# Regrouping a batch one output unit sooner, with three small moves at the start, middle and end

## The chip, the cores and the metric

The kernel runs on one core of one Trainium2 chip. The metric is the device time of one execution in microseconds (us), the median over runs. The core has TensorE (PE, matmuls; PEld is its weight load), VectorE (DVE), ScalarE (ACT), GpSimd (POOL) and SyncE (SP), and 16 DMA engines, which the queues of SP, ACT and POOL feed.

## The reference

A squared-ReLU attention, followed by a gated feed-forward block. All inputs and outputs are float32.

```
q, k, v: 8 batches x 12 heads x 448 x 64
scores = q k^T / sqrt(64);  attn = max(scores, 0)^2 / 448
x = attn v, heads side by side: 3584 tokens x 768
gate = max(x w_gate, 0);  val = x w_val        (768 -> 1536)
out = (gate * val) w_out                       (1536 -> 768)
```

## The kernel before

Everything is computed in bfloat16 with float32 sums. The matmuls mostly use quarters of the PE array (`mm4`: four matmuls of 64 rows by 64 columns side by side).

**One batch's attention.** k and q come as 448 rows of 64 numbers per head (tiles `kn`, `qn`, two of each, used in turn) and are needed transposed: tile `kqT` (`T_b`) holds k and q with the 64 numbers on the partitions, two heads one above the other (a pair). Six pairs make three quads. Scores are made in 21 tiles (seven per quad, `tile_of`), each 128x896 in two PSUM banks; `relu2` takes them out with a ReLU on ACT (line 211) and a square on DVE (line 212). When a quad's seven tiles are done, `values` multiplies them by v (tile `vn`) into `x`.

**Three ways to the transpose.** The first batch is transposed on PE into PSUM, pair by pair (`transposes`, line 201), and copied by DVE (line 202). The second is too, as three quads. From the third batch on, `dma_transposes(b, t)` is used, once for k (t = 0) and once for q (t = 1): DVE regroups the batch's tile into `kr` or `qr` (line 177), and SP issues four DMA transposes (line 180).

**The order.** Nothing is left to a scheduler: every instruction is pinned, so each engine works in the order in which the program names its instructions. The feed-forward work of one batch is the frame: 12 units of the gate and value matmuls (`gv_units`, 12 steps each) and 6 or 8 output units (`out_units`, 12 steps each, two per block of 128 tokens). `spread(units, events)` walks through the units step by step and runs an event, such as a score tile of the next batch, when its place (unit, step) has come. Events are sorted by place; those with the same place keep the order of the list. For the second batch the list of units is ten gate and value units (0 to 9) and six output units (10 to 15). Its last score tile falls on (12, 8).

**Banks.** Gate, value and output units take two PSUM banks in turn: `acc` alternates between banks 6, 7 and 4, 5. A unit can start when the ACT and DVE instructions of the unit before the last have emptied its banks: for an output unit an ACT copy (line 310) and a DVE addition (line 311). Score tiles use banks 0 to 3, and in the first batch 4 and 5 too.

**Loads.** Loads of k, q, v and the weights are issued by POOL (`dma_in`, line 116) and follow each other in its queue. `hold(b)` makes POOL copy an element of the last transposed k and q (line 431), so that what POOL issues behind it starts after these transposes. The stores of an output block are issued by SP, two per block.

**The first batch** (`first_batch`) starts with matmuls on a tile of zeros, then the transposes of the first two pairs (one bank for k and q of a pair), five more such matmuls, and the score tiles. **The end** (`out_pieces`) makes the last block in pieces of 384, 192 and 192 columns; their stores are issued by SP, POOL, and SP with ACT.

Of the kernel before, what the change touches and what calls it, by code (L numbers as in the profile page):

```python
# [10 lines left out]
BF16 = mybir.dt.bfloat16  # L11
AF = mybir.ActivationFunctionType
# [4 lines left out]
def kernel(  # L17
# [22 lines left out]
    nc = tc.nc  # L40

    B, H, S, D = q.shape
# [22 lines left out]
    banks = psum.tile([128, 8, 512], FP32, name="ps")  # L65

    HALVES = [(c, slice(c * 64, c * 64 + 64)) for c in range(2)]

    def pin(ins):
        return tc.keep_in_program_order(ins)  # L70
# [4 lines left out]
    def mm2(o, l, r, start, stop):  # L75

        for c, p in HALVES:
            mm(o[p], l[:, p], r, start, stop)
# [10 lines left out]
    ident = const.tile([128, 128], BF16, name="ident")  # L89
    pin(nc.vector.memset(ident, 0.0))  # L90
    kn_b = [const.tile([128, H, 4, D], BF16, name=f"kn{i}") for i in range(NB)]
    qn_b = [const.tile([128, H, 4, D], BF16, name=f"qn{i}") for i in range(NB)]


    def pair_of(b, slot):
        qd, c = divmod(slot, 2)
        return slot if b == 0 else qd + c * NQ
# [17 lines left out]
    def dma_in(o, i):  # L115
        pin(nc.gpsimd.dma_start(out=o, in_=i))  # L116
# [19 lines left out]
    def load_qk(b, h0=0, h1=H):  # L136
        load_nat(kn_b[b % NB], k, b, h0, h1)
        load_nat(qn_b[b % NB], q, b, h0, h1)

    def load_v(b):  # L140
        for c, p in HALVES:
            if b == 0:
                src = v[b].rearrange("(g c h) s d -> c h g s d", c=2, h=2)[c]
                dst = v_b[b % NB][p].rearrange("p (g h) i d -> p h g i d", h=2)
                parts = [(dst[:, h2], src[h2]) for h2 in range(2)]
            else:
                parts = [(v_b[b % NB][p], v[b, c * HP:c * HP + HP])]
            for dst, src in parts:
                dma_in(dst[:, :, 0:4, :], src[:, 0:256, :].rearrange("g (j i) d -> j g i d", i=4))
                dma_in(dst[:, :, 4:7, :], src[:, 256:448, :].rearrange("g (j i) d -> j g i d", i=3))  # L150
# [19 lines left out]
    T_b = [const.tile([128, 2, HP, S], BF16, name=f"kqT{i}") for i in range(NB)]  # L170

    def dma_transposes(b, t):


        n = b % NB
        nat, grp = ((kn_b[n], kr), (qn_b[n], qr))[t]
        pin(nc.vector.tensor_copy(grp.rearrange("p i (h d) -> p i h d", d=D), nat.rearrange("p h i d -> p i h d")))
        for i in range(4):
            r = 128 if i < 3 else 64
            pin(nc.sync.dma_start_transpose(out=T_b[n][:, t, :, i * 128:i * 128 + r], in_=grp[0:r, i, :]))  # L180
# [14 lines left out]
    def transposes(b, hp, bank):  # L195

        ps = bank.bitcast(BF16).rearrange("p (t c) -> p t c", t=2)
        for t, nat in enumerate((kn_b[b % NB], qn_b[b % NB])):
            for i in range(4):
                for h2, half in HALVES:  # L200
                    pin(nc.tensor.transpose(ps[half, t, i * 128:i * 128 + 128], nat[:, 2 * hp + h2, i, :], ident))  # L201
        pin(nc.vector.tensor_copy(T_b[b % NB][:, :, hp, :], ps[:, :, 0:S]))  # L202

    def transpose_quad(b, qd):
        ps = sc_later()
        for c in range(2):
            transposes(b, pair_of(b, 2 * qd + c), ps[:, c, :])

    def relu2(src, dst):
        r = rpool.tile([128, 2, S], BF16, name="r_sb")  # L210
        pin(nc.scalar.activation(r, src, AF.Relu))  # L211
        pin(nc.vector.tensor_tensor(dst, r, r, ALU.mult))  # L212
# [8 lines left out]
    def tile_of(b, n, ps):  # L221

        qd, i = divmod(n, NC)
        T = T_b[b % NB]
        a = i * 128 if i < 4 else (i - 4) * 128 + 64
        mm4([ps[:, r, :S] for r in range(2)], lambda r, c: T[:, 0, pair_of(b, 2 * qd + c), a:a + 64],
            lambda r, c: T[:, 1, pair_of(b, 2 * qd + c), :], True, True)
        return ps[:, :, :S], attn_of(b, qd)[:, 2 * i:2 * i + 2, :]

    def value_passes(b, qd, ps, i0, i1):  # L230

        attn, v_sb = attn_of(b, qd), v_b[b % NB]
        for i in range(i0, i1):
            mm4([ps[:, r, :S] for r in range(2)], lambda r, c: v_sb[:, 2 * qd + c, i, :],
                lambda r, c: attn[:, 2 * i + c, :], i == 0, i == NC - 1)

    def exchange(b, qd):
        a = slice(2 * qd, 2 * qd + 2)
        for (_, p), (_, other) in zip(HALVES, HALVES[::-1]):
            pin(nc.vector.tensor_copy(x_of[b][1][p, a, :], x_of[b][0][other, a, :]))  # L240
# [7 lines left out]
    def idle_matmuls(ps, n):  # L248

        for _ in range(n):  # L250
            mm2(ps[:, :S], blank[:, 0:128], blank, True, True)
# [29 lines left out]
    def segment_rows(b0, s):  # L281

        b, s = b0 + s // 7, s % 7
        r = out[b * S:(b + 1) * S, :]
        i, half = divmod(s, 2)
        if half:
            return r[256:448, :].rearrange("(j i) m -> i j m", i=3)[i]
        return r[0:256, :].rearrange("(j i) m -> i j m", i=4)[i]

    def store(b0, t, o_sb, c0, c1, engines):  # L290
        for s in range(2):
            pin(engines[s].dma_start(out=segment_rows(b0, 2 * t + s)[:, c0:c1],  # L292
                                     in_=o_sb[s * 64:s * 64 + 64, c0:c1]))
# [22 lines left out]
    def out_pieces(b0, t):  # L316

        hT = hT_of[b0]
        o_sb = opool.tile([128, d_model], FP32, name="o_sb")
        cuts = [0, OH, OH + OH // 2, d_model]  # L320
        turn = [acc(), acc()]
        for n, (c0, c1) in enumerate(zip(cuts, cuts[1:])):
            o_ps = turn[n % 2][:, n // 2, :c1 - c0]
            for kf in range(KF):
                mm2(o_ps, hT[:, kf, bass.ts(t, 128)], wo_sb[kf // 6][:, kf % 6, c0:c1], kf == 0, kf == KF - 1)
            pin(nc.scalar.activation(out=o_sb[:, c0:c1], in_=o_ps, func=AF.Copy))  # L326
            store(b0, t, o_sb, c0, c1, ((nc.sync, nc.sync), (nc.gpsimd, nc.gpsimd), (nc.sync, nc.scalar))[n])

    STRAIGHT = [(e, hp) for e in range(2) for hp in range(HP)]

# [32 lines left out]
    def first_batch(units):  # L363


        def passes(u, n):
            for _ in range(n):
                units[u].pop(0)()

        def bank(n):  # L370
            return banks[:, n, :]

        def tile(n, at=None):
            todo.append(tile_of(0, n, sc_first() if at is None else banks[:, at:at + 2, :]))

        todo = []

        def scored():
            relu2(*todo.pop(0))

        idle_matmuls(bank(6), 12)
        transposes(0, 0, bank(6))
        transposes(0, 1, bank(7))
        idle_matmuls(bank(4), 5)
        tile(0)
        tile(1)
        both = banks[:, 6:8, :]
        for n in range(2, 19):
            tile(n)
            if n in (3, 5, 7, 9):  # L390
                hp = n // 2 + 1
                idle_matmuls(bank(6 + hp % 2), 2)
                transposes(0, hp, bank(6 + hp % 2))
            if n in (12, 17):
                value_passes(0, n // 14, both, 0, NC)
            scored()
            if n in (12, 17):
                qd = n // 14
                pin(nc.vector.tensor_copy(x_of[0][0][:, 2 * qd:2 * qd + 2, :], both[:, :, :S]))  # L399
        tile(19)  # L400
        scored()
        passes(0, 4)
        scored()
        tile(20, 0)
        scored()
        value_passes(0, 2, both, 0, 4)
        scored()
        passes(1, 4)
        value_passes(0, 2, both, 4, NC)
        exchange(0, 0)  # L410
        exchange(0, 1)
        pin(nc.scalar.activation(x_of[0][0][:, 4:6, :], both[:, :, :S], AF.Copy))
        exchange(0, 2)
        for n in range(4):
            for u in range(2):
                passes(u, 2)
# [4 lines left out]
    def values_event(b, qd):  # L421
        return lambda: values(b, qd, sc_later())
# [4 lines left out]
    def hold(b):  # L427

        flag = const.tile([128, 2], BF16, name="flag")
        for t in range(2):  # L430
            pin(nc.gpsimd.tensor_copy(flag[:, t:t + 1], T_b[b % NB][:, t, HP - 1, S - 1:S]))
# [20 lines left out]
    def evenly(units, u0, u1, events):  # L452
# [6 lines left out]
    units = gv_units(0)  # L459
    first_batch(units)  # L460
    load_qk(2)
    load_v(2)
    new_x(1)
    units = units[2:] + out_units(0)
    todo = events_of(1)
    spread(units, [(2, 6, transposes_event(1, 0)), (2, 6, transposes_event(1, 1)), (2, 10, transposes_event(1, 2)),
                   (3, 0, todo.pop(0))] + evenly(units, 3, 13, todo) +
           [(13, 8, lambda: dma_transposes(2, 0)), (14, 2, values_event(1, 2)),
            (14, 8, lambda: dma_transposes(2, 1)), (14, 8, lambda: hold(2))])
    for b in range(2, B):  # L470
        new_x(b)
        units = gv_units(b - 1) + out_units(b - 1)
# [37 lines left out]
```

## Time and profile before

| | us |
|---|---|
| median of 3 runs (420.43 to 422.28) | 421.97 |
| the profiled execution | 420.63 |
| its span, first to last instruction | 418.9 |
| PE busy in the span (98%) | 409.2 |
| DVE busy (58%) | 243.2 |
| ACT busy (56%) | 236.6 |
| POOL busy (15%) | 60.8 |

The times of single instructions below come from the profiled execution, which took 1.73 us more than its span. The granted clock of TensorE was 1.000. In the profile's lines the first two numbers are the start and the duration in us; "x4" is a number of instructions that were merged; the bracket at the end tells how long the engine was idle before, and what ended that. SPq and ACTq are the engines' DMA issues. In the table of windows the columns are the stretch, its length, the busy time (with the number of instructions) of PE, PEld, DVE, ACT and POOL, the granted clock, the share of the DMA engines and GB/s.

### The profile page before, as it was taken

How to read it: one execution, taken by the hardware profiler on the slowest of the kernel's cores; microseconds unless marked ns; L12 is line 12 of the kernel's file. 1: busy time of each engine (PE TensorE's matmuls, PEld its weight loads, DVE VectorE, ACT ScalarE, POOL GpSimd, SP SyncE). 2: the span in 40 equal slices, each digit the busy share in tenths (PEclk: the TensorE clock that was granted, in tenths of full speed). 3: DMA queues.
4: the chain of work that ended last, by engine and by line, in shares of the span. 5: the costliest groups of instructions: out<-in, count | busy, mean ns of one | idle time of the engine just before them, and what ended most of it. 6: DMA issues, size and time to landing. Idle time of an engine off the chain costs nothing.

```text
span 418.9 us, 19287 instructions
## 1 busy us (share of the span) xinstructions
PE 409.2 (98%) x8858; PEld 355.3 (85%) x8858; DVE 243.2 (58%) x422; ACT 236.6 (56%) x345; POOL 60.8 (15%) x93
## 2 busy tenths in 40 slices
PE   8899999999999999999999999999999999999996
PEld 4467677877887778877788899999999999999995
DVE  4985677436765666557565576557565555642221
ACT  3962886256764666565664756656555666632222
POOL 8823500053005000320004000020000000000001
PEclk9999999999999999999999999999999999999999
DMA  9999999789959960596316972271504100130014
GB/s 159 182 200 196 201 207 196 131 141 194 162 132 144 147 120 4 104 189 92 69 41 122 191 85 56 55 129 40 98 12 108 39 3 4 40 79 2 3 41 115
DMA packets 86033, 44.33 MB, mean 106 GB/s; under 512 B 54304, under 2 KB 82464, under 8 KB 85952
## 3 DMA queue, kind: packets, MB, share of 16 engines
q0 software_dynamic: 46976, 23.47, 42.7%
q1 hardware_dynamic: 38624, 19.39, 22.7%
q8 instruction: 69, 1.13, 1.1%
q10 hardware_dynamic: 352, 0.25, 0.2%
q14 instruction: 12, 0.10, 0.1%
HBM read 47.19 MB, written 11.01 MB: 139 GB/s over the span
## 4 chain that ended last, share of the span: by engine, by line
PE 91%; DVE 4%; DMA 2%; SPq 1%; issue 0%; ACT 0%; POOL 0%; POOLq 0%; DVEq 0%
PE ps L73 90%; DVE attn L212 2%; PE ps L201 1%; DMA kr<-in_k_dram 1%; SPq L180 1%; DMA kqT<-qr 1%; DVE kqT L202 1%; DVE x L399 0%; ACT r_sb L211 0%; DVE x L240 0%; DVE hT L278 0%; DVE kn L128 0%; POOL out_dram L292 0%; ACT g_sb L277 0%; POOLq L505 0%
## 5 line engine op out<-in xcount | busy, mean ns | idle before, releaser
L73 PE MATMUL ps<-x,gv 64*64 64x448 bf16 x4608 | 242.7, 349 | 0.4 <-ACT r_sb L211 0.3
L73 PEld LDWEIGHTS <-gv 64*64 64x64 bf16 x4608 | 192.7, 107 | 28.7 <-issue 2.1
L211 ACT ACTIVATE r_sb<-ps 128x896 bf16<-128x896 f32 x168 | 151.5, 924 | 56.8 <-PE ps L73 53.1
L212 DVE TENSOR_TENSOR attn<-r_sb 128x896 bf16<-128x896 bf16 x168 | 103.8, 624 | 80.0 <-ACT r_sb L211 79.6
L73 PE MATMUL ps<-wo,hT 64*64 64x384 bf16 (+2 forms) x2664 | 123.3, 321 | 0.8 <-issue 0.8
L73 PEld LDWEIGHTS <-hT 64*64 64x64 bf16 (+1 forms) x2664 | 105.2, 107 | 9.6 <-issue 1.6
L278 DVE TENSOR_TENSOR hT<-ps,g_sb 128x448 bf16<-128x448 f32 x96 | 59.7, 622 | 44.6 <-ACT g_sb L277 42.8
L277 ACT ACTIVATE g_sb<-ps 128x448 bf16<-128x448 f32 x96 | 51.9, 542 | 56.8 <-PE ps L73 56.2
L73 PE MATMUL ps<-kqT 64*64 64x448 bf16 x672 | 70.2, 351 | 3.3 <-ACT r_sb L211 2.2
L116 POOL DMA_DIRECT2D vn<-in_v_dram x36 | 23.4, 667 | 171.9 <-PE ps L73 156.1
L310 ACT ACTIVATE o_sb<-ps 128x384 f32<-128x384 f32 x54 | 26.4, 489 | 29.8 <-PE ps L73 29.3
L311 DVE TENSOR_TENSOR o_sb<-ps,o_sb 128x384 f32<-128x384 f32 x54 | 30.0, 555 | 19.7 <-ACT o_sb L310 19.4
L73 PEld LDWEIGHTS <-kqT 64*64 64x64 bf16 x672 | 29.7, 107 | 10.4 <-issue 3.7
L73 PE MATMUL ps<-attn,vn 64*64 64x448 bf16 x672 | 37.9, 349 | 0.0
L73 PEld LDWEIGHTS <-vn 64*64 64x64 bf16 x672 | 27.6, 107 | 4.2 <-issue 0.3
L244 ACT ACTIVATE x<-ps 128x448 bf16<-128x448 f32 x21 | 11.4, 544 | 29.8 <-PE ps L73 29.8
L245 DVE CAST x<-ps 128x448 bf16<-128x448 f32 x21 | 13.1, 625 | 15.4 <-PE ps L73 15.4
L240 DVE COPY x<-x 64x896 bf16<-64x896 bf16 x48 | 20.0, 417 | 2.7
L292 POOL DMA_DIRECT2D out_dram<-o_sb x2 | 1.1, 560 | 139.7 <-ACT o_sb L326 139.7
L116 POOL DMA_DIRECT2D qn<-in_q_dram x20 | 14.8, 762 | 3.2 <-DVE attn L212 1.8
L116 POOL DMA_DIRECT2D kn<-in_k_dram x16 | 12.1, 772 | 2.0 <-DVE attn L212 1.0
L73 PE MATMUL ps<-blank 128*64 128x448 bf16 x50 | 8.1, 466 | 1.2 <-DVE blank L88 1.2
(28 smaller groups left out, 58.0 us busy)
## 6 DMA issues: line engine op xcount, KB each, us to landing
out_dram<-o_sb SPq DMA_DIRECT2D x54, 192.0 KB, 3.4
kn<-in_k_dram POOLq DMA_DIRECT2D x7, 384.0 KB, 9.9
qn<-in_q_dram POOLq DMA_DIRECT2D x7, 384.0 KB, 12.2
vn<-in_v_dram POOLq DMA_DIRECT2D x14, 192.0 KB, 7.1
wo<-in_moe_w_out_dram POOLq DMA_DIRECT2D x2, 1152.0 KB, 16.7
kn<-in_k_dram POOLq DMA_DIRECT2D x7, 288.0 KB, 10.7
qn<-in_q_dram POOLq DMA_DIRECT2D x7, 288.0 KB, 13.2
vn<-in_v_dram POOLq DMA_DIRECT2D x14, 144.0 KB, 7.2
```

What stands on the lines that cost most here:

```text
L73: pin(nc.tensor.matmul(o, lhsT=l, rhs=r, start=start, stop=stop, skip_group_check=True))
L116: pin(nc.gpsimd.dma_start(out=o, in_=i))
L180: pin(nc.sync.dma_start_transpose(out=T_b[n][:, t, :, i * 128:i * 128 + r], in_=grp[0:r, i, :]))
L211: pin(nc.scalar.activation(r, src, AF.Relu))
L212: pin(nc.vector.tensor_tensor(dst, r, r, ALU.mult))
L240: pin(nc.vector.tensor_copy(x_of[b][1][p, a, :], x_of[b][0][other, a, :]))
L244: pin(nc.scalar.activation(x_of[b][0][:, 2 * qd, :], ps[:, 0, :S], AF.Copy))
L245: pin(nc.vector.tensor_copy(x_of[b][0][:, 2 * qd + 1, :], ps[:, 1, :S]))
L277: pin(nc.scalar.activation(g_sb, o[0], AF.Relu, scale=float(out_scale)))
L278: pin(nc.vector.tensor_tensor(hT[:, mf, col:col + S], o[1], g_sb, ALU.mult))
L310: pin(nc.scalar.activation(state[t][:, m], o[0], AF.Copy))
L311: pin(nc.vector.tensor_tensor(state[t][:, m], o[1], state[t][:, m], ALU.add))
```

## The change

Four things change.

1. The first two pairs are transposed by a new function. It uses a bank for each of the four groups (k and q of pair 0, k and q of pair 1; banks 6, 7, 5, 4), and copies each group by itself: three by DVE, and the k of pair 1 by ACT. Four idle matmuls in bank 2 follow, instead of five in bank 4.
2. In the second batch's frame, the regrouping and the DMA transposes of the third batch move: k from place (13, 8) to (12, 8), q from (14, 8) to (13, 6).
3. The load of the third batch's v is issued behind `hold(2)`, instead of right after the loads of its k and q.
4. The stores of the middle piece at the very end are issued by SP and ACT instead of POOL.

```diff
+    def first_transposes(numbers):
+
+        for n, (hp, t) in zip(numbers, ((0, 0), (0, 1), (1, 0), (1, 1))):
+            ps = banks[:, n, :].bitcast(BF16)
+            for i in range(4):
+                for h2, half in HALVES:
+                    pin(nc.tensor.transpose(ps[half, i * 128:i * 128 + 128],
+                                            (kn_b, qn_b)[t][0][:, 2 * hp + h2, i, :], ident))
+            o = T_b[0][:, t, hp, :]
+            if (hp, t) == (1, 0):
+                pin(nc.scalar.activation(o, ps[:, 0:S], AF.Copy))
+            else:
+                pin(nc.vector.tensor_copy(o, ps[:, 0:S]))
...
-            store(b0, t, o_sb, c0, c1, ((nc.sync, nc.sync), (nc.gpsimd, nc.gpsimd), (nc.sync, nc.scalar))[n])
+            store(b0, t, o_sb, c0, c1, ((nc.sync, nc.sync), (nc.sync, nc.scalar), (nc.sync, nc.scalar))[n])
...
-        transposes(0, 0, bank(6))
-        transposes(0, 1, bank(7))
-        idle_matmuls(bank(4), 5)
+        first_transposes((6, 7, 5, 4))
+        idle_matmuls(bank(2), 4)
...
     load_qk(2)
-    load_v(2)
     new_x(1)
...
-           [(13, 8, lambda: dma_transposes(2, 0)), (14, 2, values_event(1, 2)),
-            (14, 8, lambda: dma_transposes(2, 1)), (14, 8, lambda: hold(2))])
+           [(12, 8, lambda: dma_transposes(2, 0)), (13, 6, lambda: dma_transposes(2, 1)),
+            (14, 2, values_event(1, 2)), (14, 8, lambda: hold(2)), (14, 8, lambda: load_v(2))])
```

## The prediction

> **What bounds the kernel now.** I read the profiled execution first: 420.63 us, of which 418.9 us are the span and 1.73 us lie around it. Then the page, the chain of waits, the stages, and the timeline of the three places that the change touches. TensorE (PE) is busy 98% of the span, so only its few idle stretches can be gained. The stages, from the table of windows (us, PE busy, weight loads):
>
> ```profile
> 8.21:27.36 19.15, 16.44 (x284) 9.69 (x283) 16.54 (x30) 17.50 (x22) 11.95 (x17) 1.00 1.34 190
> ...
> 100.00:400.00 300.00, 300.00 (x6639) 272.79 (x6635) 175.49 (x301) 173.63 (x255) 20.25 (x29) 1.00 0.50 82
> ```
>
> From 100 to 400 us PE never stops, at a granted clock of 1.00: what is won or lost before 100 us arrives at the end undiminished, and nothing changes in between. The change acts in three stretches, so I read each from the timeline. The start:
>
> ```profile
> 6.93 1.16 DVE L202 COPY kqT<-ps 128x896 bf16<-128x896 bf16 x2 [0.72 <-PE ps L201]
> 7.11 0.73 PEld L73 LDWEIGHTS <-blank 128*64 128x64 bf16 x10
> 8.21 0.51 PEld L73 LDWEIGHTS <-kqT 64*64 64x64 bf16 x13 [0.36 <-DVE kqT L202]
> 8.64 17.11 ACT L211 ACTIVATE r_sb<-ps 128x896 bf16<-128x896 f32 x21 [5.26 <-PE ps L73]
> ```
>
> The first scores wait for two copies of 896 columns, and from 8.64 to 25.75 ACT works without a gap: an earlier first score moves this whole stage. The regrouping of the third batch:
>
> ```profile
> 70.36 0.63 DVE L212 TENSOR_TENSOR attn<-r_sb 128x896 bf16<-128x896 bf16 x1 [0.99 <-ACT r_sb L211]
> 70.90 0.55 DVE L311 TENSOR_TENSOR o_sb<-ps,o_sb 128x384 f32<-128x384 f32 x1
> 71.36 0.95 DVE L177 COPY kr<-kn 128x3072 bf16<-128x3072 bf16 x1
> 71.81 1.37 PEld L73 LDWEIGHTS <-vn 64*64 64x64 bf16 x28
> 72.39 5.98 SPq L180 DMA_TRANSPOSE kqT<-kr  x4
> 75.20 0.96 DVE L177 COPY qr<-qn 128x3072 bf16<-128x3072 bf16 x1
> 78.41 1.23 SPq L292 DMA_DIRECT2D out_dram<-o_sb  x2
> 79.75 7.41 SPq L180 DMA_TRANSPOSE kqT<-qr  x4
> 88.39 0.38 PE L73 MATMUL ps<-kqT 64*64 64x448 bf16 x4 [1.04 <-DMA kqT<-qr]
> ```
>
> The copies on VectorE (DVE) are short; SP's queue is the long part. Its four k transposes, a store and four q transposes follow one another from 72.39 to 87.16, the last lands at 88.25, and the batch's first score waits 1.04 us for it. The end, from the timeline:
>
> ```profile
> 414.68 1.10 POOL L292 DMA_DIRECT2D out_dram<-o_sb  x2 [139.66 <-ACT o_sb L326]
> 415.40 0.54 ACTq L292 DMA_DIRECT2D out_dram<-o_sb  x1
> ```
>
> and the engines' drains in the rows of the kernel's last line (ns shortest/median/longest, then first and last start):
>
> ```profile
> L505 POOLq DRAIN x3: 46/93/2938, 415.1 to 418.6; - x3
> L505 SPq DRAIN x3: 7/7/13, 417.9 to 418.3; - x3
> ```
>
> POOL's drain of 2.94 us, begun at about 415.1, ends at about 418.05; SP, which waits for the other stores, drains at 417.9. POOL is last by some 0.15 us.
>
> **First quad in four banks.** The 32 transposes stay; PE finishes the four groups of eight at about 6.58 (k0), 6.88 (q0), 7.11 (k1) and 7.34 (q1). Two copies of 620 ns become four of half the width. No row has this half copy. From above it costs 620 ns (as if width cost nothing), from below 310 ns. DVE copies of 64x896 (417 ns) and 128x3072 (951 ns) give a fixed part of about 0.20 us, so half of the rest, 0.21, makes 0.41 us; I take it, as the same engine and type, with 0.33 us from start to start, since neighbouring DVE rows overlap by 0.08. Then k0 is copied at 6.63 to 7.04, q0 at 6.96 to 7.37, q1 at 7.39 to 7.80. ACT copies k1, idle then, at 7.16 to 7.70 (its 128x448 copy takes 544 ns). The last copy ends at 7.80 instead of 8.09: **-0.28 us**. The idle matmuls, one pair per 0.187 us from 7.17, end at 7.92 with four and 8.10 with five, so the removed one is needed for this, and bounds it too. At the two bounds the edit gives -0.39 and +0.24. ACT's chain moves along; the loads that the next transposes use (q of heads 4 to 7, issued at 4.35 and 5.0 us, about 4.6 us to landing) are there 0.2 us before they would be wanted; later loads have more.
>
> **Regrouping one unit sooner.** On PE's order the k copy moves from step (13,8) to (12,8), behind the last score of the second batch, which stands at the same step and ahead of it in the list. On DVE that is only 0.46 us: the copy starts at 70.90, when the multiply of line 212 is done, instead of 71.36. But it now stands ahead of unit 12's addition (line 311), which it pushes from 70.90 to 71.76, ending at 72.32. Unit 14 accumulates in the bank that this addition frees. It starts at 71.65 (its eight weight loads of 0.0425 us lie before 71.81, a matmul 0.18 behind) and touches the second half-bank 0.08 later, at 71.73. Before, the bank was free at 71.45, with 0.28 us to spare; now it is free at about 72.36, and PE waits **+0.63 us** with all that is queued behind. Bounds: 0, if DVE gets to the addition first after all, and 0.86, the copy less the overlap. The q copy at (13,6) runs at 72.23 to 73.19 and pushes unit 13's addition to 73.7; its bank is wanted by unit 15 at about 75, so this is free. The values' cast (73.66 before) comes after PE's delay, so that is free as well.
>
> On SP the k transposes start at 71.93; the q transposes follow them directly, the store of unit 13 and the gap around it (1.38 us) now behind them. They start at 77.95 instead of 79.75, and the last lands at 77.95 + 5.27 (to its issue) + 3.24 = 86.46. The first score wants them at 87.35 + 0.63 = 87.98: 1.5 us to spare, and the 1.04 us wait goes: **-1.04 us** (bound 0, if they land late). Unit 13's store leaves about 8 us later; three output buffers are there, and the next is written after 112 us: nothing.
>
> **Values behind the transposes.** Four issues on POOL (2.63 us, from the later batches' rows) move from 49 to 63 us to behind the two flag copies, at about 86.7. Before, the k and q loads stood ahead of them in the same queue and landed at 64 to 69 us, so the copies at 70.9 and 72.2 still find their data. Behind them now stand the k, q and v loads of the fourth batch. From 88.79 on these landed 384 KB at 94.4 and then 288 KB every 1.5 us: 3.6 us of lead, then 0.19 MB/us. So the third batch's values (672 KB) land at about 93.8, wanted at 102; the fourth batch's k at 97.3, wanted by its copy at 102.0; its q at 100.8, wanted at 106.1. Cost **0**, with about 4 us of cover at the thinnest, PE being some 0.7 earlier by then. Without cover DVE, and with it PE, waits for the whole lateness. The two PE waits put down to "issue" (0.49 at 68.18, 0.32 at 74.27), in time with heavy DMA, I leave: 0, bounds -0.81 and +0.3.
>
> **Last stores.** SP and ACT issue the second piece at 414.43 in 0.47 and 0.54 us; ACT is free at 414.97, before its last copy is due at 415.04; SP's earlier stores are out by 414.6. What is left is the third piece, unchanged, and SP's end at 417.9: **-0.1 us**, between -0.15 and +0.1 if ACT is late. Issue to landing is 1.9 us for POOL's stores and 1.9 to 2.2 for those of SP and ACT: the rows show no slower path. [...]
>
> **Sum:** -0.28 + 0.63 - 1.04 - 0.10 = -0.79: 420.63 becomes 419.84 us. The profiled execution was 1.34 us under the median of the runs shown, 421.97; on that scale the forecast is 421.2.
>
> **Rivals.**
> (a) The addition does not hold PE: DVE's order or a bank free earlier. Then -1.42, 420.55 on the scale of the median. For it: only 0.28 us of slack decides, read from pipelined rows. Against it: DVE keeps its program order.
> (b) The wait stays, because transposes are slow: the fourth batch's took 8.16 and 6.83 us with loads in flight; at 8.16 for k the last lands at 71.93 + 8.16 + 0.1 + 5.1 + 3.24 = 88.5, 0.55 us late. Then -0.24, 421.7. Against: no load is in flight then.
> (c) The "issue" waits go with the removed traffic: -0.79 - 0.81 = -1.6, 420.4; with (a) as well -2.2, 419.7.
> (d) Slower: the held loads come late. Place: DVE's k copy for the fourth batch, which stands in DVE's order ahead of the multiplies that PE's values need. It decides if k lands later than 102. For it: k loads have taken 19.1 us behind a full queue; issued at 89.3, that is 108.4, PE stops 6.4 us, and the time is 421.2 + 6.4 = 427.6. Against: the queue is empty at 86.7, and the nearest rows, in the same place, took 5.6 to 9.3 us.
>
> **How the numbers follow.** About 0.5%, 2.1 us, is what a measurement of this kernel can tell from no change. Forecast 0.57, (a) 0.15, (b) 0.10, (c) 0.12, (d) 0.06. The runs before lie from 420.43 to 422.28, so a median of three can shift by some 0.7 either way. Faster by over 0.5% needs (a) and (c) together, or (c) and a lucky median: 0.10. Slower by over 0.5% is (d) and a little else: 0.07. The rest, 0.83, is no change. Range 419.4 to 422.8: down to (a) with (c), up to (b) with the start's bad bound (+0.5) and the spread of the medians; (d) is left out.
>
> **What would show it.** Right: ACT's first ReLU at about 8.36 instead of 8.64; a PE wait of about 0.6 us near 71.5 whose releaser is DVE's addition of line 311; SP's eight transposes with no store between; no wait on a transposed tile near 87; POOL's four value loads just after its flag copies; a last POOL drain no longer behind SP's. Wrong: DVE waiting for the k load near 102 us (d), a wait on line 180's tile (b), or any idle PE between 100 and 400 us.

## The result: 0.4% slower

| | before | changed |
|---|---|---|
| median of 22 runs each (us) | 421.64 (420.43 to 422.53) | 422.91 (421.41 to 430.7) |
| the profiled execution | 420.63 | 424.51 |
| its span | 418.9 | 422.7 |

The ratio is 1.004, with a 95% interval of 1.0025 to 1.0055: 1.7 us slower (1.1 to 2.3), where 0.8 us faster was forecast. The ratio leaves out one disturbed execution (430.7) and is close to that of the means of the others; the medians alone differ by 0.3%. The changed kernel also scatters more, and its profiled execution is one of the longer ones, 1.6 us over the median; it shows more of the loss than a usual run has.

### The profile page after: what moved, and what is told of

Read it like the earlier page. It is cut to its first block, busy times and chain, and to the rows that moved or that the text cites. A ratio compares the mean times of both kernels' runs of the same rounds, so it can differ in the third digit from the quotient of the medians.

```text
span 422.7 us, 19288 instructions
## 1 busy us (share of the span) xinstructions
PE 409.8 (97%) x8856; PEld 322.6 (76%) x8856; DVE 242.0 (57%) x423; ACT 237.9 (56%) x346; POOL 59.8 (14%) x91
## 3 DMA queue, kind: packets, MB, share of 16 engines
q8 instruction: 69, 1.13, 1.1%
## 4 chain that ended last, share of the span: by engine, by line
PE 93%; DVE 3%; issue 1%; DMA 1%; ACT 1%; ACTq 0%; POOL 0%; DVEq 0%; POOLq 0%
PE ps L73 91%; DVE attn L226 2%; DMA qn<-in_q_dram 1%; PE ps L201 1%; ACT r_sb L225 1%; DVE kqT L202 1%; DVE x L412 0%; DVE kr L177 0%; PE ps L210 0%; ACT o_sb L340 0%; ACTq L306 0%; DVE o_sb L325 0%; POOL qn L116 0%; DVEq L177 0%; DVEq L325 0%
## 5 line engine op out<-in xcount | busy, mean ns | idle before, releaser
L73 PEld LDWEIGHTS <-gv 64*64 64x64 bf16 x4608 | 180.2, 107 | 48.9 <-issue 2.6
L73 PE MATMUL ps<-wo,hT 64*64 64x384 bf16 (+2 forms) x2664 | 125.7, 321 | 3.7 <-issue 3.5
L73 PEld LDWEIGHTS <-hT 64*64 64x64 bf16 (+1 forms) x2664 | 100.4, 107 | 22.1 <-issue 5.3
L73 PE MATMUL ps<-kqT 64*64 64x448 bf16 x672 | 81.5, 350 | 2.3 <-ACT r_sb L225 2.2
L73 PEld LDWEIGHTS <-kqT 64*64 64x64 bf16 x672 | 36.8, 107 | 10.8 <-issue 3.7
L73 PE MATMUL ps<-attn,vn 64*64 64x448 bf16 x672 | 39.6, 349 | 0.0
L202 DVE COPY kqT<-ps 128x896 bf16<-128x896 bf16 x10 | 5.9, 620 | 2.6 <-PE ps L201 2.6
```

The costliest lines, as they stand in the source:

```text
L73: pin(nc.tensor.matmul(o, lhsT=l, rhs=r, start=start, stop=stop, skip_group_check=True))
```

## The profile after

The chain's shares (part 4 of the page of the changed kernel) hardly differ from before; what is new is 1% "issue". From the timeline of the changed kernel, the start:

```profile
7.33 0.41 PE L210 MATMUL ps<-ident,qn 128*64 128x128 bf16 x8 [0.99 <-DMA qn<-in_q_dram]
7.79 0.84 DVE L216 COPY kqT<-ps 128x448 bf16<-128x448 bf16 x2 [1.00 <-PE ps L210]
8.01 0.54 ACT L214 ACTIVATE kqT<-ps 128x448 bf16<-128x448 bf16 x1 [4.63 <-PE ps L210]
9.32 17.11 ACT L225 ACTIVATE r_sb<-ps 128x896 bf16<-128x896 f32 x21 [0.77 <-PE ps L73]
```

The copies cost what was forecast (one on DVE 0.39 us, forecast 0.41; the one on ACT 0.54), but in this execution the first q load landed at 7.2 us and the transposes of q waited for it. The first ReLU starts at 9.32, 0.68 later than in the profile of before. The regrouping:

```profile
72.20 0.95 DVE L177 COPY kr<-kn 128x3072 bf16<-128x3072 bf16 x1
73.06 0.55 DVE L325 TENSOR_TENSOR o_sb<-ps,o_sb 128x384 f32<-128x384 f32 x1
73.30 6.08 SPq L180 DMA_TRANSPOSE kqT<-kr  x4
73.67 0.51 PE L73 MATMUL ps<-wo,hT 64*64 64x384 bf16 x6 [0.26 <-DVE o_sb L325]
79.42 6.14 SPq L180 DMA_TRANSPOSE kqT<-qr  x4
87.24 2.62 POOL L116 DMA_DIRECT2D vn<-in_v_dram  x4 [0.30 <-issue]
88.41 0.51 PE L73 MATMUL ps<-kqT 64*64 64x448 bf16 x4
```

The k copy stands ahead of the addition, and PE waits for that (the 0.26 in the bracket counts from matmul ends that the profile models). By the places of the work, the values' matmuls behind it start 1.89 us later than before (73.86 against 71.97), and 1.42 of that is there already at the last score tile (70.28 against 68.86): the addition costs about 0.5. SP's eight transposes follow each other, and the score at 88.41 waits for nothing. At that point both kernels are level (88.39 before), in spite of the late start. Then:

```profile
110.63 10.97 SPq L180 DMA_TRANSPOSE kqT<-qr  x4
112.92 1.46 PE L73 MATMUL ps<-wo,hT 64*64 64x384 bf16 x29 [1.03 <-issue]
120.48 1.29 PE L73 MATMUL ps<-wo,hT 64*64 64x384 bf16 x25 [1.93 <-issue]
```

PE stands still twice, for 1.03 and 1.93 us, and the profile names nobody that it waits for. These 2.96 us are most of the 3.8 by which the span grew. Compared matmul by matmul, counted from the last one back, the changed kernel is 0.1 us behind at 108 us and 3.5 us at 122. In the profile of before PE has no wait between 100 and 400 us. The four q transposes of the fourth batch take 10.97 us; before, their line was

```profile
111.30 6.83 SPq L180 DMA_TRANSPOSE kqT<-qr  x4
```

The DMA queues between 113 and 118 us, before and then changed (packets, MB, and the time of the packets as a share of 16 engines' time; packets that overlap can bring it over 100%):

```profile
q1 hardware_dynamic: 3340, 0.81, 110.1%
q8 instruction: 2, 0.03, 3.1%
```

```profile
q1 hardware_dynamic: 1601, 0.39, 74.6%
q0 software_dynamic: 1199, 0.51, 77.8%
q8 instruction: 1, 0.02, 1.2%
```

Before, POOL's loads (q0) were over by then, and SP's queue (q1) moved 0.81 MB. Now the loads are still running (0.51 MB on q0), SP's queue moves 0.39 MB, and the instruction queue (q8) one packet instead of two.

**What PE waits for.** The table of windows counts the instructions up to a moment, so it tells how many PE and PEld instructions had run when a wait began. For the two waits of the changed kernel:

```profile
0.00:112.91 112.91, 105.90 (x2139) 80.83 (x2140) 73.23 (x132) 68.34 (x94) 40.33 (x63) 1.00 1.22 173
0.00:120.47 120.47, 111.53 (x2267) 85.64 (x2268) 77.26 (x139) 71.59 (x99) 40.33 (x63) 1.00 1.23 172
```

2139 + 2140 = 4279 and 2267 + 2268 = 4535, just 256 apart. The same sum for such waits, in this kernel and in those of the experiments:

```
kernel                    wait ends at (us)        instructions      modulo 256
before                     68.67,  74.59           2489, 2745        185, 185
changed                    45.88,  70.11           1465, 2489        185, 185
changed                   112.92, 120.48           4279, 4535        183, 183
c_values                  119.10, 125.84           4536, 4792        184, 184
f_twice                   120.45, 127.75           4536, 4792        184, 184
e_hold4                   159.12                   6325              181
```

In each of these the wait lies at nearly the same count modulo 256 (181 to 185). It goes by the count and not by the work, as the two waits behind 2489 instructions show:

```profile
68.67 0.51 PE L73 MATMUL ps<-wo,hT 64*64 64x384 bf16 x6 [0.49 <-issue]
70.11 0.36 PE L73 MATMUL ps<-wo,hT 64*64 64x384 bf16 x4 [0.51 <-issue]
```

Before, six matmuls are left ahead of the next score tile, in the changed kernel four ahead of the same tile: it has two idle matmuls and their two weight loads less at its start, so the same count falls two matmuls further on in the work. The packets of the instruction queue q8 are about 16 KB each (69 of them with 1.13 MB), and PE's 17,716 matmuls and weight loads in before make 69.2 times 256. The one packet that q8 moved between 113 and 121 us started between 117.6 and 117.7; PE stood still from 118.55 to 120.48. The counts are read here as blocks: one packet brings 256 of PE's instructions, and in these waits PE stands still until its next block is there. That is an inference, since no row of the profile names what ended the waits. From 113 to 118 us, POOL's loads (q0, 77.8%) and SP's transposes (q1, 74.6%) kept the DMA engines busy in every slice. Both together did not always bring a wait: between 103 and 113 us before, with 1.17 MB on q0 and 0.46 MB on q1, PE never stopped.

## The experiments

**Each part alone.** Theory 1: the moved values load makes PE wait for instructions. Theory 2: the first quad costs the time. Theory 3: the addition behind the copy does. Four kernels, each the kernel before with one part of the change.

a_first, the new transposes of the first quad (the new function is the one shown in the change):

```diff
-        transposes(0, 0, bank(6))
-        transposes(0, 1, bank(7))
-        idle_matmuls(bank(4), 5)
+        first_transposes((6, 7, 5, 4))
+        idle_matmuls(bank(2), 4)
```

> Only the first quad's transposes in four banks. Theory 1 (the loss is PE waiting for instructions, because the third batch's values now load beside later loads and transposes): nothing of it is in this kernel, so the time is 0.0 to 0.4 us under before, the first ReLU at 8.3 to 8.6 if the first q load has landed by 6.3 us, as in the profile of before. Theory 2 (the first quad's new order makes the first scores later, 9.32 instead of 8.64): 0.5 to 0.8 us slower, first ReLU at about 9.3.

421.84 against 421.43 us, ratio 1.0009 (0.9994 to 1.0025). The first ReLU starts at 8.36, as forecast, but nothing is left of it at the end. PE is 0.28 us ahead of before until 43 us and 0.13 behind at 50: between them lies a wait for instructions of 0.32 us (ends at 44.65) that the profile of before doesn't have. The wait for the transposed tile near 88 us is 1.44 us instead of 1.04, but that is not the new transposes' doing: without them it is 1.36 in d_stores, 1.45 in f_twice and 1.54 in c_values. Not theory 2, and not the gain of theory 1 either.

b_regroup, the regrouping sooner:

```diff
-           [(13, 8, lambda: dma_transposes(2, 0)), (14, 2, values_event(1, 2)),
-            (14, 8, lambda: dma_transposes(2, 1)), (14, 8, lambda: hold(2))])
+           [(12, 8, lambda: dma_transposes(2, 0)), (13, 6, lambda: dma_transposes(2, 1)),
+            (14, 2, values_event(1, 2)), (14, 8, lambda: hold(2))])
```

> Only the regrouping sooner; the values load stays where it was. Theory 1: the wait for the transposed tiles near 88 us is gone, unit 14 waits about 0.6 us for the addition, no PE wait for instructions between 100 and 125 us: 0.4 to 1.0 us faster than before. Theory 3 (the addition behind the copy is the cause): 0.5 us slower or more, PE idle near 73 us.

420.44 against 421.43, ratio 0.9971 (0.9955 to 0.9986): 1.2 us faster. From its timeline:

```profile
72.73 0.51 PE L73 MATMUL ps<-wo,hT 64*64 64x384 bf16 x6 [0.39 <-DVE o_sb L311]
85.77 0.19 POOL L431 COPY flag<-kqT 128x1 bf16<-128x1 bf16 x1 [5.79 <-DMA kqT<-qr]
```

The wait for the addition is there, the one near 88 us is gone, and after 100 us there is none. So the addition is not what makes the change slower.

c_values, the values load behind the flag copies:

```diff
     load_qk(2)
-    load_v(2)
...
-            (14, 8, lambda: dma_transposes(2, 1)), (14, 8, lambda: hold(2))])
+            (14, 8, lambda: dma_transposes(2, 1)), (14, 8, lambda: hold(2)), (14, 8, lambda: load_v(2))])
```

> Only the values load behind the two flag copies; the regrouping stays where it was, so the loads start even later (about 89 us) than with the whole change. Theory 1: PE waits put down to issue of 1 to 3 us between 105 and 125 us, and 1 to 3 us slower than before. Theories 2 and 3: the same time as before within 0.4 us.

424.27 against 421.43, ratio 1.0059 (1.0036 to 1.0081): 2.5 us slower, as theory 1 has it, without the gain that the regrouping brings to the whole change. Its timeline:

```profile
111.53 10.95 SPq L180 DMA_TRANSPOSE kqT<-qr  x4
119.10 1.32 PE L73 MATMUL ps<-wo,hT 64*64 64x384 bf16 x26 [1.66 <-issue]
125.84 0.38 PE L73 MATMUL ps<-kqT 64*64 64x448 bf16 x2 [1.24 <-issue]
```

d_stores, the middle piece's stores:

```diff
-            store(b0, t, o_sb, c0, c1, ((nc.sync, nc.sync), (nc.gpsimd, nc.gpsimd), (nc.sync, nc.scalar))[n])
+            store(b0, t, o_sb, c0, c1, ((nc.sync, nc.sync), (nc.sync, nc.scalar), (nc.sync, nc.scalar))[n])
```

> Only the middle piece's stores by SP and ACT. All theories: ACT's last copy 0.3 us later after the last matmul than in before (its DMA issue and what follows it stand ahead), POOL's last drain short; the span from the last matmul's end the same within 0.2 us, and the time the same within 0.3 us.

421.51 against 421.43, ratio 0.9994 (0.9977 to 1.0012). POOL's drain at the end is gone from the last step (what is left of it begins at 419.2 us, behind SP's at 419.0), and the span ends 3.87 us after the start of ACT's last copy (415.95), against 3.81 before (415.04). That copy was not late here: it follows ACT's copy of the piece before by 1.00 us, as before (0.99), and so it is in k_stores below. In the profiles of the whole change, e_hold4 and g_oldvalues it follows by 1.29, as expected; why only there stays open.

So theory 1 is left. Is it the bytes still in flight that count, or the place of the values load? Two kernels ask that, and two look at the rest; these four ran on another chip.

e_hold4, the whole change, with the loads of the fifth batch's k and q (and what follows them in POOL's queue) held:

```diff
+    def after_x(b):
+        flag = const.tile([128, 1], BF16, name="seen")
+        pin(nc.gpsimd.tensor_copy(flag, x_of[b][1][:, HP - 1, S - 1:S]))
...
-            events.append((0, 1, lambda: (load_qk(b + 1), load_v(b + 1))))
+            events.append((0, 1, lambda: (after_x(2) if b == 3 else None, load_qk(b + 1), load_v(b + 1))))
```

> The whole change, with the k and q loads of the fifth batch (and what POOL issues behind them) held until the third batch's last x is written, near 129 us: the same bytes, but none of them between 112 and 129 us. Theory 1 (PE's instruction blocks come late while loads and transposes share the DMA engines during the output units): no PE wait put down to issue between 105 and 128 us, q transposes of the fourth batch in 6 to 7 us instead of 10.97, and 2 to 3 us less than the whole change, so 1 us under before. Rival 4 (the waits come with the transposes alone, or from the order of the loads, not from the load that is still in flight): waits near 112 and 120 us stay, time 422 to 423.

422.21 against 421.46, ratio 1.0018 (0.9997 to 1.0038). The first half came as expected: from 100 to 130 us PE is busy all the time, and the q transposes take 6.32 us. The gain did not: the loads now fall on the next batch's transposes, and so does the wait.

```profile
108.92 6.32 SPq L180 DMA_TRANSPOSE kqT<-qr  x4
152.62 8.12 SPq L180 DMA_TRANSPOSE kqT<-qr  x4
159.12 0.38 PE L73 MATMUL ps<-x,gv 64*64 64x448 bf16 x2 [2.03 <-issue]
```

PE stood still from 157.1. Between 147 and 155 us, with loads and transposes together, the instruction queue had moved a single packet:

```profile
q0 software_dynamic: 1896, 0.81, 87.4%
q1 hardware_dynamic: 1867, 0.46, 58.5%
q8 instruction: 1, 0.02, 0.7%
```

The wait went to where loads and transposes now ran together. Rival 4, the transposes alone, finds no support: from about 108 to 115 us they ran without loads beside them here (0.95 MB on q1, nothing on q0), and PE did not wait. The wait is not all that PE lost there: the granted clock, 1.00 up to it, was 0.57 between 159 and 163 us (0.99 over 130 to 400 us, 0.996 over the whole execution), and counted by place PE fell 4.0 us behind. Why the clock fell is not shown; behind the waits of f_twice, the next experiment, it stayed at 1.00.

f_twice, the kernel before with 672 KB more in the queue:

```diff
-            events.append((0, 1, lambda: (load_qk(b + 1), load_v(b + 1))))
+            events.append((0, 1, lambda: (load_qk(b + 1), load_v(b + 1), load_v(b + 1) if b == 2 else None)))
```

> The kernel before, with the fourth batch's values loaded twice (the second time the same bytes into the same tile): 672 KB more in POOL's queue ahead of the fifth batch's k and q, nothing else moved. Theory 1: the load queue stays full about 4 us longer, to 114 us or later, PE waits put down to issue between 105 and 128 us, 1 to 3 us slower than before, as with the values load moved. Rival 4 (the place of the third batch's values itself does it): the time of before within 0.5 us.

426.03 against 421.46, ratio 1.0098 (1.0071 to 1.0126): 4.1 us slower, with two waits that sum to 4.0.

```profile
120.45 1.32 PE L73 MATMUL ps<-wo,hT 64*64 64x384 bf16 x26 [2.21 <-issue]
127.75 0.38 PE L73 MATMUL ps<-kqT 64*64 64x448 bf16 x2 [1.79 <-issue]
```

Nothing of the change is in this kernel; a longer queue of loads at that place is enough. It costs more than expected (1 to 3).

g_oldvalues, the whole change but for the values load:

```diff
+    load_v(2)
...
-            (14, 2, values_event(1, 2)), (14, 8, lambda: hold(2)), (14, 8, lambda: load_v(2))])
+            (14, 2, values_event(1, 2)), (14, 8, lambda: hold(2))])
```

> The whole change without the move of the values load. Theory 1: as regrouping alone (420.4) plus what the first quad and the stores bring, 420.0 to 420.7; no PE wait for instructions over 0.5 us after 100 us. Theory 2 (the first quad's order costs): 421 or more.

421.34 against 421.46, ratio 0.9994 (0.9975 to 1.0013). The loss of the whole change is gone, but the gain of regrouping was not to be seen: a miss, since 420.0 to 420.7 was expected. In its profile the first ReLU is early (8.45), then the transposes wait 0.56 us at 11.08 for q of heads 4 to 7.

i_best, the whole change with the values load and the last stores as before, and the k copy behind the addition:

```diff
-            store(b0, t, o_sb, c0, c1, ((nc.sync, nc.sync), (nc.sync, nc.scalar), (nc.sync, nc.scalar))[n])
+            store(b0, t, o_sb, c0, c1, ((nc.sync, nc.sync), (nc.gpsimd, nc.gpsimd), (nc.sync, nc.scalar))[n])
...
+    load_v(2)
...
-           [(12, 8, lambda: dma_transposes(2, 0)), (13, 6, lambda: dma_transposes(2, 1)),
-            (14, 2, values_event(1, 2)), (14, 8, lambda: hold(2)), (14, 8, lambda: load_v(2))])
+           [(13, 0, lambda: dma_transposes(2, 0)), (13, 6, lambda: dma_transposes(2, 1)),
+            (14, 2, values_event(1, 2)), (14, 8, lambda: hold(2))])
```

> The first quad in four banks; the k copy at place (13, 0), behind unit 12's addition, and the q copy at (13, 6); values load and last stores as before. All theories with the 0.6 us wait for the addition: no PE wait near 72 us on the addition; the last transpose lands at about 87.0, wanted at about 87.3, so the wait near 88 us is 0 to 0.5; 419.6 to 420.4, the fastest so far. If the addition was not the cause of that wait, 420.4 or more.

421.34 against 421.46, ratio 0.9994 (0.9973 to 1.0015). No wait for the addition, but one of 0.94 us for the transposed tile at 88.87 (0 to 0.5 was expected), and five waits put down to issue that sum to 1.79 us. A miss.

These two left it open whether the first quad or the stores take regrouping's gain away, so four kernels ran beside each other on a third chip: regrouping alone again (l_again), with the first quad (j_first), with the stores (k_stores), and with the places of i_best (m_behind); the edits are those above.

> Regrouping alone once more, beside the next three on one chip. If its gain holds on another chip: 0.2 to 0.4% faster than before, no PE wait for instructions over 0.5 us after 100 us.

421.23 against 421.43, ratio 0.9978 (0.9953 to 1.0003). The interval holds 1, and the expectation of no wait over 0.5 us missed: this profile has a wait of 1.66 us for instructions that ends at 117.88, which the first profile of the same kernel did not have. The same kernel can have the wait in one execution and not in another; here the fifth batch's q landed at 114.5 us, there at 112.2.

> Regrouping and the first quad in four banks, values load and stores as before. If the first quad takes away what regrouping brings (as the difference between 420.44 alone and 421.34 with first quad and stores suggests): 0.5 to 1.0 us slower than regrouping alone, with PE waits for the q load near 11 us or for instructions. If that difference lay in the chip: 0.0 to 0.3 us faster than regrouping alone.

420.35, ratio 0.9972 (0.9950 to 0.9994), where regrouping alone had 0.9978: no loss by the first quad is to be seen, and a gain or loss of a few tenths of a us would not show. Why g_oldvalues and i_best gained nothing stays open.

> Regrouping and the last stores by SP and ACT. As regrouping alone within 0.2 us, if the stores are worth nothing; 0.5 us slower or more, if they are what takes the gain away.

420.16, ratio 0.9964 (0.9941 to 0.9987), the fastest kernel of all, though not by more than the intervals.

> Regrouping with the k copy at place (13, 0), behind unit 12's addition, and the q copy at (13, 6); all else as before. No PE wait on the addition near 72 us (0.4 to 0.6 less); the last transpose 0.5 later than with regrouping alone. If it is still in time: 0.3 to 0.6 us faster than regrouping alone. If not, the wait near 88 us is back by up to 1 us and nothing is won.

420.48, ratio 0.9971 (0.9948 to 0.9995). PE does not wait for the addition, and waits 0.85 us near 88 us again:

```profile
71.08 0.55 DVE L311 TENSOR_TENSOR o_sb<-ps,o_sb 128x384 f32<-128x384 f32 x1
71.55 0.95 DVE L177 COPY kr<-kn 128x3072 bf16<-128x3072 bf16 x1
88.36 0.38 PE L73 MATMUL ps<-kqT 64*64 64x448 bf16 x4 [0.85 <-DMA kqT<-qr]
```

The two waits trade against each other, as the second branch of the expectation has it.

**All profiles together.** The 14 profiles differ in when the last of the fifth batch's q landed, and PE's waits for instructions between 100 and 130 us go with that:

| last q of the fifth batch landed (us) | profiles | waits for instructions, sum (us) |
|---|---|---|
| held until later | e_hold4 | 0 |
| 112.2 to 114.0 | b_regroup, before, g_oldvalues, d_stores, a_first, m_behind | 0 to 0.25 |
| 114.4 to 115.1 | j_first, l_again, i_best, k_stores | 0.24 to 1.92 |
| 120.5 to 128.0 | changed, c_values, f_twice | 2.90 to 4.00 |

## Why the prediction was wrong

- **Values behind the transposes: cost 0.** This is the step that failed. It followed the bytes to the copies that need them, and there it was right: k of the fourth batch landed at 99.8 us (97.3 was forecast) and was copied at 102.03 with no wait, as before. It did not follow the queue to its end, and took for granted that between 100 and 400 us, where PE had never stopped, nothing changes. The 672 KB pushed every later load back, so that the fifth batch's k and q, over by about 113 us before, ran until about 118 (the last landed at 120.5), beside the fourth batch's q transposes. No wait in the profile names those loads; but while they ran beside the transposes PE stood still for 1.03 and 1.93 us, and from 113 to 118 us the instruction queue moved one packet, where it had moved two before. That the loads held its packets up is the author's reading: the order of loads and waits in the runs fits it, no row shows it. Rival (d) had the late loads, but the wrong one waiting for them.
- **The "issue" waits: 0, bounds -0.81 and +0.3.** The same error as a term of the sum. They were seen "in time with heavy DMA", and the load moved was weighed at the place it left, not at the place it went to. The term measured 2.96 us in the profile after; alone in c_values the moved load costs 2.5 us (1.5 to 3.4). Rival (c) tied these waits to the traffic, but reckoned only with their going; they came where the traffic went. The instruction counts of the two waits of before, just 256 apart (2489 and 2745), were a sign of what they are.
- **Regrouping: +0.63 and -1.04.** Right in mechanism: by place, the addition costs 0.47 us in the changed kernel and 0.59 in b_regroup, and there is no wait near 88. By itself the regrouping is worth 1.2 us (0.6 to 1.9), more than the 0.41 forecast. Matmul by matmul, b_regroup's profile shows from where: 0.6 lost at the addition, 1.3 won at the wait near 88, and 0.5 won at the instruction wait that ends at 74.59 before and is not there in this profile. This last part was not in the forecast; such waits come and go (0.59 us near 75 us in a_first and f_twice, none there in c_values and d_stores), and no run shows that the regrouping is what removed it. From 92 to 400 us its lead stays the same, so nothing later adds to it.
- **First quad: -0.28.** The first ReLU came 0.28 earlier alone (8.36) and 0.68 later in the whole change's profile. The prediction took the q load as landed; it lands at about the time it is wanted (the transposes of q waited for it until 6.60 us in b_regroup and 7.33 in the changed kernel, and not at all in before, at 6.36). k_stores, without the new transposes, waits for this load too (until 7.38), so its lateness is not theirs. Where it is in time, the head start is spent at the next q load (g_oldvalues, 11.08) or at a wait for instructions (a_first, 44.65). Measured alone: +0.1% with an interval that holds 0.
- **Stores: -0.1.** Nothing to be measured (0.9994 and, beside regrouping, 0.9964 against 0.9978 alone).
- **The range** ended at 422.8 and the changed kernel's median is 422.91: the waits that cost were not among the cases.

The sum of the parts alone, -1.2 + 2.5 + 0.4 - 0.3 = 1.4 us, agrees with the 1.7 of the whole change within the intervals.

## What to carry to other kernels

A moved load has two ends to check: who reads its bytes, and what the rest of its queue now runs beside. Idle stretches of an engine that no semaphore explains should be counted in instructions: here such waits began at counts that differ by 256 (2489 and 2745 before, 4279 and 4535 in the changed kernel), and that led to the instruction queue and to the loads and DMA transposes that ran together ahead of the long ones. Of the places tried for the loads, the one that had the fifth batch's q landed sooner was the better one (before, landed at 113.2 us, at 421.43 and 421.46 us, against c_values at 424.27 and f_twice at 426.03, where it landed at 120.5 us or later), although no wait in the profiles names that load; e_hold4 shows that holding a load can also just move it to the next transposes.

## What was not expected of the hardware

PE stood still for up to 2.21 us (f_twice) at nearly the same count modulo 256 (181 to 185) where POOL's loads and SP's DMA transposes had run together; with the transposes alone (108 to 115 us in e_hold4) it did not, nor with both together between 103 and 113 us before. With loads alone the waits were short: 0.49 us at 68.67 before, 0.32 at 45.88 in the changed kernel, with no transpose on the queues in the 5 us ahead. The issue of one DMA transpose took 1.29 us in the median and up to 3.96 us beside loads (the first of the four issued from 110.63 us on in the changed kernel). The same kernel can have such a wait in one execution and not in the next (none after 100 us and 1.66 us in the two profiles of regrouping alone). Right behind a wait of 2.03 us the granted clock was 0.57 for 4 us in one execution (e_hold4); it was 1.00 for the 4 us behind the wait of 1.93 us in the changed kernel, and 1.00 between 100 and 130 us in f_twice, with waits of 2.21 and 1.79 us.
